# Reordering the opening of a fused attention and feed-forward kernel: two weights loaded and converted ahead of k and v

## The chip, the cores and the metric

The kernel runs on one core of a Trainium2 chip. The metric is the device time of one execution in microseconds. Before the change the median of three runs is 1489.09 us (1489.03 to 1489.66).

## The reference

Three layers follow one another on 4608 tokens (8 batches of 576) of width 512 (8 heads of 64), all in fp32:

```
kv  = einsum('bhsd,bhse->bhde', k, v)            # one 64x64 matrix per batch and head
out = einsum('bhsd,bhde->bhse', q, kv)
x   = out / sqrt(mean(out*out, -1) + 1e-6) * g_norm      # per token and head
h   = maximum(maximum(x @ w1, x @ w2), x @ w3)           # 512 -> 768
x   = h @ w_out                                          # 768 -> 512
xn  = x / sqrt(mean(x*x, -1) + 1e-6) * rms_g
y   = (silu(xn @ w_gate) * (xn @ w_val)) @ w_out2        # 512 -> 1536 -> 512
```

## The kernel before, in words

Tokens are worked in nine tiles of 512, called t, each cut into four token tiles of 128, called i (token tiles 0 to 3 make t = 0, 4 to 7 make t = 1). Every large product is made of three fp32r products (high x high, high x low, low x high), so each weight and each activation is held as a high and a low part. A unit of the second layer, `proj`, is 4 x 3 products of 512 columns into one PSUM bank.

The weights arrive as raw 64-bit words of 512 KB for each 128x512 block, and are converted on the core. One conversion, `convert1`, runs through these steps; a generator's `yield` stands between two of them:

1. `conv_a` (lines 90 to 99): a clip of the high words on VectorE or GpSimd (line 96; which one is chosen by the running number `n` of the conversion), and a copy of the low words on ScalarE (line 97).
2. A scaling on ScalarE (line 116).
3. A shift on VectorE (line 120).
4. Two VectorE passes, the sign and the sum with the low words (lines 122 and 123).
5. A copy on ScalarE, which gives the high part (line 126).
6. A subtraction on VectorE, which gives the low part (line 128).

`convert` has the same work in fewer steps and gives the last subtraction to GpSimd (lines 81 and 82, 101, 107 to 109); `convert2` likewise (lines 239 to 246). The list `todo` holds the weights in the order w1, w2, w3 of block j = 0, the same of j = 1 and then the block 0 of `wo`, and so on. `start` issues the load of the next one on SP's queue and puts it in `flight`; `pump` takes every weight in flight one step further and starts one more. `con(c0, c1, ...)` takes the named ones one step each.

A token tile has five steps (`token_steps`, called by `go((i, step), ...)`):

0. Products of q with the batch's k-v matrix on TensorE (line 367), squares on ScalarE (line 373).
1. Sums of the squares by head on VectorE (line 377), their mean (line 379), and the power -1/2 on GpSimd (line 381).
2. The scaling of the products, `xn`, on VectorE (line 344).
3. Four transposes on TensorE (line 387) and the high part of x on ScalarE (line 388).
4. The low part of x on VectorE (line 393).

`do_kv(b)` makes the k-v matrices of batch b from four chunks of 128 tokens and a tail of 64 (line 332), and copies them out of PSUM on VectorE (lines 336 and 337). Its argument `idle` and the function `busy` put products of the identity on TensorE that nothing reads (line 315).

`do_p(t, j, mid, p, last)` makes one hidden block of 128 rows: three units with the weights w1, w2, w3 of block j; a copy of the first on ScalarE (line 437), a max on VectorE after the second and the third (lines 441 and 445), and the split of the hidden block (ScalarE line 428, GpSimd line 429). `mid` is called after the first and after the second unit, `last` at the end: that is where the token steps and the conversions of other tiles are written in. `do_o` multiplies a hidden block with a block of `wo`.

The order of the instructions on every engine is that of the program text (`manual_schedule`); an engine waits at the head of its list. The opening, from line 992 on, is written out by hand: k and v of batch 0, q, three weights, k and v of batch 1, q, three weights are loaded; then come the k-v products of batch 0, the tokens 0 to 3 with the conversions of c0, c1, c2 (the three weights of j = 0) between them, the first unit of t = 0 in two halves of 256 tokens (`p0`), and then `do_p(0, 0)`, `do_p(0, 1)`, `do_o`, `do_p(1, 0)`, and a loop over j from 2 on.

Of the kernel before, what the change touches and what calls it, by code (L numbers as in the profile page):

```python
# [18 lines left out]
P = 128  # L19
# [12 lines left out]


@with_exitstack
def tile_kernel(ctx: ExitStack, tc, qT, k, v, gcol, w1, w2, w3, wo, wg, wv, wo2, rmsg, out):
    nc = tc.nc
    w1, w2, w3, wo, wg, wv, wo2 = (w.bitcast(I32) for w in (w1, w2, w3, wo, wg, wv, wo2))

# [14 lines left out]
    def unit(shape, dt, name):  # L53
        return up.tile(shape, dt, tag="u", name=name)
# [35 lines left out]
    def conv_a(raw):  # L90
        lo, hi = raw[:, :, 0], raw[:, :, 1]
        tt = unit([P, 2, 512], F32, "wt")
        n_w[0] += 1
        n = n_w[0]
        eng = nc.gpsimd if n > 3 and n % 2 else nc.vector
        eng.tensor_scalar(tt[:, 0], f32(hi), TOP, -TOP, ALU.min, ALU.max)
        nc.scalar.activation(tt[:, 1].bitcast(I32), lo.bitcast(U32), AF.Copy, scale=2.0**-29)
        return tt
# [178 lines left out]
    def cols(w, j):  # L277
        return w[j]

    for j in range(J1 + 1):  # L280
        if j < J1:
            todo += [(convert2 if j >= 3 else convert if j else convert1)((1, i, j), cols(w, j)) for i, w in enumerate((w1, w2, w3))]
        if j:
            todo.append((convert2 if j >= 3 else convert)((1, "o", j - 1), wo[(j - 1) * P:j * P, :]))

    KV = {}
    Q = {}
# [2 lines left out]
    def load_kv_part(b, c):  # L290
        r = b * S
        m, tail = KV.setdefault(b, ([None] * 4, []))
        for i, (src, nm) in enumerate(((k, "k"), (v, "v"))):
            if c == 2:
                tail.append(rp.tile([P, 512], F32, tag="raw", name="kvt"))
                nc.sync.dma_start(tail[i][:64], src[r + 512:r + 576, :])
            else:
                m[2 * i + c] = unit([P, 2, 512], F32, nm)
                rows = src[r + 2 * c * P:r + 2 * (c + 1) * P, :]
                nc.sync.dma_start(m[2 * i + c], rows.rearrange("(p two) f -> p two f", two=2))  # L300

    def load_kv(b):
        for c in range(3):
# [13 lines left out]
    def do_kv(b, kvb, idle={}):  # L317
        m, tail = KV.pop(b)
        pk = psum([P, NP, D], "pk")
        for c in range(5):  # L320
            if c in idle:
                busy(idle[c])
            for hp in range(NP):
                for h in range(2):
                    o = (2 * hp + h) * D
                    if c < 4:
                        kk = m[c // 2][:, c % 2, o:o + D]
                        vv = m[2 + c // 2][:, c % 2, o:o + D]
                    else:
                        kk = tail[0][:64, o:o + D]  # L330
                        vv = tail[1][:64, o:o + D]
                    nc.tensor.matmul(  # L332
                        pk[h * D:(h + 1) * D, hp, :], kk, vv,
                        start=(c == 0 and hp == 0), stop=(c == 4), skip_group_check=True,
                    )
        nc.vector.tensor_copy(kvb[:D, :, 0:D], pk[:D])
        nc.vector.tensor_copy(kvb[D:, :, D:], pk[D:])
        kvbd[b] = kvb

    XN = {}  # L340
# [10 lines left out]

    X = {}

    def token_steps(i, pool=ps):

        st = {}

        def products():
            q = Q[i // 2]
            o = (i % 2) * P  # L360
            po = st["po"] = pool.tile([P, DM], F32, tag="ps" if pool is ps else "acc", name="po")
            t0 = i * P
            b = t0 // S
            n = min(P, (b + 1) * S - t0)
            for hp in range(NP):
                f = slice(hp * P, (hp + 1) * P)
                nc.tensor.matmul(po[:n, f], q[:, hp, o:o + n], kvbd[b][:, hp, :], start=True, stop=True)  # L367
                if n < P:
                    nc.tensor.matmul(po[n:, f], q[:, hp, o + n:o + P], kvbd[b + 1][:, hp, :], start=True, stop=True)
            if i % 2:  # L370
                del Q[i // 2]
            st["sq"] = tmp("sq")
            nc.scalar.activation(st["sq"], po, AF.Square)

        def scales():
            ss = sp.tile([P, H], F32, tag="ss", name="ss")
            nc.vector.tensor_reduce(ss, st["sq"].rearrange("p (h d) -> p h d", h=H), AX.X, ALU.add)
            ms = sp.tile([P, H], F32, tag="ms", name="ms")
            nc.vector.tensor_scalar(ms, ss, 1.0 / D, EPS, ALU.mult, ALU.add)  # L379
            st["rs"] = sp.tile([P, H], F32, tag="rs", name="rs")  # L380
# [609 lines left out]
                pass  # L990

    with tc.manual_schedule():
        load_kv(0)
        load_q(0)
        load_q(1)
        for _ in range(3):
            start(todo[0])
        nc.sync.dma_start(gc, gcol)
        load_kv(1)
        load_q(2)  # L1000
        load_q(3)
        for _ in range(3):
            start(todo[0])
        make_identity(nc, ident)
        nc.gpsimd.memset(mhalf, -0.5)
# [2 lines left out]
        z = unit([P, 2, NP, P], F32, "kvbd")  # L1008
        nc.gpsimd.memset(z, 0.0)
        kvb += [z[:, 0], z[:, 1]]  # L1010
        c0, c1, c2 = flight[:3]
        tok = [token_steps(i) for i in range(NS)] + [token_steps(i, pa) for i in range(NS, 2 * NS)]

        def go(*steps):
            for i, n in steps:
# [3 lines left out]
            for g in gs:  # L1019
                next(g, 0)  # L1020

        do_kv(0, kvb[0], {0: 11, 2: 6})
        busy(4)
        new_x(0)
        go((0, 0), (1, 0), (0, 1), (1, 1), (2, 0))
        con(c0)
        go((3, 0))
        con(c0)
        go((2, 1), (0, 2))
        busy(8)  # L1030
        go((0, 3))
        con(c0, c0)
        go((1, 2), (3, 1))
        busy(5)
        go((1, 3))
        con(c1, c0)
        go((0, 4), (1, 4))
        con(c0, c1)
        p0 = pa.tile([P, TB], F32, tag="acc", name="p0")
        half = TB // 2  # L1040
        busy(4)
        proj(p0, W[1, 0, 0], X[0], 0, half)
        go((2, 2), (3, 2), (2, 3), (3, 3))
        busy(3)
        con(c1, c1)
        go((2, 4), (3, 4))
        con(c1, c2, c1, c2, c2, c2, c2, c2)
        proj(p0, W[1, 0, 0], X[0], half, TB)
        del flight[:3]
        pump(2)  # L1050
        nc.sync.dma_start(gb, rmsg)

        n_mid = [0]

        def mid():
            n_mid[0] += 1
            if n_mid[0] == 1:
                do_kv(1, kvb[1])
                pump()
            elif n_mid[0] == 2:  # L1060
                pump()
                go((4, 0), (5, 0), (4, 1), (5, 1))
            elif n_mid[0] == 3:
                go((6, 0), (7, 0))
            elif n_mid[0] == 4:
                go((4, 2), (6, 1), (5, 2), (7, 1))
                pump()
            elif n_mid[0] == 5:
                go((4, 3), (6, 2))
            else:  # L1070
                go((4, 4), (5, 3), (7, 2), (6, 3))


        do_p(0, 0, mid, p0, mid)
        new_x(1)
        do_p(0, 1, mid, None, mid)
        do_o(1, 0, 0, J1, lambda: go((7, 3), (5, 4), (6, 4), (7, 4)))
        pump()
        do_p(1, 0, pump)

        def pumped():
            tick()
# [123 lines left out]
                down(n, ph, xs)  # L1206


_INS = ["qT", "k", "v", "gcol", "w1", "w2", "w3", "wo", "wg", "wv", "wo2", "rmsg"]


# [34 lines left out]
```

## Time and profile before

| | before |
|---|---|
| median of 3 runs | 1489.09 us |
| profiled execution, its own time | 1492.71 us |
| span of the profiled execution | 1490.7 us |
| TensorE busy | 1472.2 us (99%) |
| VectorE busy | 951.2 us (64%) |
| ScalarE busy | 574.5 us (39%) |
| GpSimd busy | 527.1 us (35%) |
| mean rate of the DMA queues | 211 GB/s |

The busy time of TensorE counts every product, also the ones that nothing reads. The time of an execution is a little longer than its span, and the profiled execution is longer than the median of the runs. In the profile PE is TensorE, DVE is VectorE, ACT is ScalarE, POOL is GpSimd and SP is SyncE, whose queue issues the loads and stores. A clock of 1.00 is 2.4 GHz at TensorE, 0.50 is 1.2 GHz.

### The profile page before, as it was taken

How to read it: one execution, taken by the hardware profiler on the slowest of the kernel's cores; microseconds unless marked ns; L12 is line 12 of the kernel's file. 1: busy time of each engine (PE TensorE's matmuls, PEld its weight loads, DVE VectorE, ACT ScalarE, POOL GpSimd, SP SyncE). 2: the span in 40 equal slices, each digit the busy share in tenths (PEclk: the TensorE clock that was granted, in tenths of full speed). 3: DMA queues.
4: the chain of work that ended last, by engine and by line, in shares of the span. 5: the costliest groups of instructions: out<-in, count | busy, mean ns of one | idle time of the engine just before them, and what ended most of it. 6: DMA issues, size and time to landing. Idle time of an engine off the chain costs nothing.

```text
span 1490.7 us, 20078 instructions
## 1 busy us (share of the span) xinstructions
PE 1472.2 (99%) x7282; PEld 1221.9 (82%) x7282; DVE 951.2 (64%) x1376; ACT 574.5 (39%) x1027; POOL 527.1 (35%) x402
## 2 busy tenths in 40 slices
PE   8899999999999999999999999999999999999998
PEld 7788888888888878888888888888888888888887
DVE  5895476798777966832353655764756656755756
ACT  3553343444343524321232442443333432434432
POOL 2554234334343434311141422532424422443323
PEclk9999999999999999999999999999999999999999
DMA  9323244677547664517695843784657844775442
GB/s 353 104 67 133 65 155 170 219 256 256 201 161 263 245 222 161 192 56 295 240 364 190 329 171 127 303 327 175 242 193 285 304 187 186 282 265 215 179 173 107
DMA packets 104866, 313.80 MB, mean 211 GB/s; under 512 B 11840, under 2 KB 11840, under 8 KB 104768
## 3 DMA queue, kind: packets, MB, share of 16 engines
q1 hardware_dynamic: 104768, 312.52, 57.2%
q8 instruction: 58, 0.95, 0.3%
q14 instruction: 40, 0.33, 0.1%
HBM read 239.08 MB, written 73.40 MB: 210 GB/s over the span
## 4 chain that ended last, share of the span: by engine, by line
PE 92%; DVE 4%; DMA 1%; issue 1%; POOL 1%; ACT 1%; SPq 0%; DVEq 0%; POOLq 0%
PE ua L789 18%; PE da L789 9%; PE ub L789 9%; PE p L410 9%; PE p L412 9%; PE p L411 9%; PE db L789 4%; PE uc L789 4%; PE acc L412 4%; PE acc L410 4%; PE acc L411 4%; PE dc L789 2%; PE po L367 2%; PE pk L332 1%; PE pt L387 1%
## 5 line engine op out<-in xcount | busy, mean ns | idle before, releaser
L410 PE MATMUL p<-x,w 128*128 128x512 f32 (+1 forms) x652 | 257.7, 395 | 1.6 <-ACT w L126 1.0
L411 PE MATMUL p<-x,w 128*128 128x512 f32 (+1 forms) x652 | 253.3, 389 | 1.6 <-DVE x L393 1.6
L412 PE MATMUL p<-x,w 128*128 128x512 f32 (+1 forms) x652 | 253.8, 389 | 0.2 <-DVE w L128 0.2
L789 PE MATMUL ua<-xo,w 128*128 128x512 f32 x864 | 213.4, 389 | 0.0
L429 POOL TENSOR_TENSOR ho<-sl,ho 128x512 fp32r<-128x512 f32 x72 | 98.1, 1369 | 303.3 <-issue 265.0
L789 PEld LDWEIGHTS ua<-xo,w 128*128 128x128 f32 x864 | 162.2, 188 | 33.6
L429 POOL TENSOR_TENSOR hs<-h,hs 128x512 fp32r<-128x512 f32 x54 | 75.8, 1403 | 292.5 <-ACT hs L428 276.5
L429 POOL TENSOR_TENSOR ho<-t,ho 128x512 fp32r<-128x512 f32 x96 | 123.8, 1293 | 133.1 <-ACT ho L428 116.1
L789 PE MATMUL ub<-xo,w 128*128 128x512 f32 x576 | 146.1, 389 | 0.0
L411 PEld LDWEIGHTS p<-x,w 128*128 128x128 f32 x652 | 122.6, 188 | 26.6 <-DVE x L393 2.6
L412 PEld LDWEIGHTS p<-x,w 128*128 128x128 f32 x652 | 122.4, 188 | 26.7 <-POOL w L246 0.4
L410 PEld LDWEIGHTS p<-x,w 128*128 128x128 f32 x652 | 122.5, 188 | 26.4 <-ACT w L126 1.1
L789 PEld LDWEIGHTS ub<-xo,w 128*128 128x128 f32 x576 | 108.1, 188 | 22.4
L871 ACT ACTIVATE s<-ua 128x512 f32<-128x512 f32 x96 | 57.2, 596 | 139.1 <-PE ua L789 139.0
L789 PE MATMUL da<-ho,wd 128*128 128x512 f32 x432 | 105.7, 389 | 0.0
L381 POOL TENSOR_TENSOR rs<-ms,mhalf 128x8 f32<-128x8 f32 x36 | 64.2, 1794 | 105.0 <-DVE ms L379 104.8
L428 ACT ACTIVATE ho<-t 128x512 fp32r<-128x512 f32 x96 | 59.4, 627 | 100.5 <-DVE t L623 100.5
L428 ACT ACTIVATE hs<-h 128x512 fp32r<-128x512 f32 x54 | 34.1, 632 | 163.5 <-DVE h L445 148.7
L789 PEld LDWEIGHTS da<-ho,wd 128*128 128x128 f32 x432 | 81.1, 188 | 16.8
L441 DVE TENSOR_TENSOR s<-p,s 128x512 f32<-128x512 f32 x54 | 37.2, 688 | 83.0 <-PE p L412 83.0
L819 DVE TENSOR_TENSOR c<-uc,s 128x512 f32<-128x512 f32 x48 | 33.1, 690 | 83.8 <-PE uc L789 83.8
L410 PE MATMUL acc<-hs,w 128*128 128x512 f32 x216 | 85.6, 396 | 0.0
(147 smaller groups left out, 2828.2 us busy)
## 6 DMA issues: line engine op xcount, KB each, us to landing
w<-wd SPq DMA_DIRECT2D x180, 512.0 KB, 8.0
wd<-ws SPq DMA_DIRECT2D x72, 512.0 KB, 3.0
wd<-wd SPq DMA_DIRECT2D x72, 512.0 KB, 7.4
wq<-wd SPq DMA_DIRECT2D x72, 256.0 KB, 8.3
xo<-td SPq DMA_DIRECT2D x32, 512.0 KB, 9.6
q<-in_qT SPq DMA_DIRECT2D x18, 512.0 KB, 5.5
raw<-in_w SPq DMA_DIRECT2D x18, 512.0 KB, 9.0
raw<-in_wo SPq DMA_DIRECT2D x18, 512.0 KB, 5.1
```

The lines of the kernel that those rows point to most:

```text
L332: nc.tensor.matmul(pk[h * D:(h + 1) * D, hp, :], kk, vv, start=(c == 0 and hp == 0), stop=(c == 4), skip_group_check=True,)
L367: nc.tensor.matmul(po[:n, f], q[:, hp, o:o + n], kvbd[b][:, hp, :], start=True, stop=True)
L381: nc.gpsimd.tensor_tensor(st["rs"], ms, mhalf.to_broadcast([P, H]), ALU.pow)
L410: nc.tensor.matmul(o, ah, bh, start=first, stop=False)
L411: nc.tensor.matmul(o, ah, bl, start=False, stop=False)
L412: nc.tensor.matmul(o, al, bh, start=False, stop=last)
L428: nc.scalar.activation(hs[:, 0], h, AF.Copy)
L429: nc.gpsimd.tensor_tensor(hs[:, 1], h, f32(hs[:, 0]), ALU.subtract)
L441: nc.vector.tensor_tensor(s2, p, s1, ALU.max)
L789: nc.tensor.matmul(o, aa, bb, start=first and q == 0, stop=last and q == 2, skip_group_check=True)
L819: nc.vector.tensor_tensor(t, p, s, ALU.add)
L871: nc.scalar.activation(t, p, AF.Copy)
```

## The change

- The first two weights (c0 and c1) are loaded ahead of k and v of batch 0, and converted ahead of the k-v products. The third follows behind q; four more are loaded behind batch 1 (before: three).
- The 64-token tails of k and v of batches 0 and 1 come in one transfer, `kvt`, a new input of 128 rows of 1024 values that the host lays out; batch 0 uses its partitions 0 to 63, batch 1 the others.
- The k-v matrices are copied out of PSUM by ScalarE, for all batches.
- Token tiles 4 to 7 take their squares head by head, eight ScalarE instructions of 64 columns that also give the sum (`accum_out`), and VectorE's sums are left out for them.
- The weights d0, d1, d2 (j = 1), o0 and p1[0] to p1[2] (j = 2) are `convert1`, and their steps are written out in `mid`, as are those of the token tiles 4 to 7. The first ten conversions clip on VectorE (before: the first three, and every second one after them).
- The k-v products of batch 1 stand ahead of the second half of p0 (before: after it). The first unit of t = 1 is made in two halves, and `do_p(1, 0)` stands ahead of the first `do_o`.
- More products that nothing reads stand ahead of and between the first k-v products.

The diff, without the lines of the host and of the arguments:

```diff
-        eng = nc.gpsimd if n > 3 and n % 2 else nc.vector
+        eng = nc.gpsimd if n > 10 and n % 2 else nc.vector
...
-            todo += [(convert2 if j >= 3 else convert if j else convert1)((1, i, j), cols(w, j)) for i, w in enumerate((w1, w2, w3))]
+            todo += [(convert2 if j >= 3 else convert1)((1, i, j), cols(w, j)) for i, w in enumerate((w1, w2, w3))]
         if j:
-            todo.append((convert2 if j >= 3 else convert)((1, "o", j - 1), wo[(j - 1) * P:j * P, :]))
+            todo.append((convert2 if j >= 3 else convert if j > 1 else convert1)((1, "o", j - 1), wo[(j - 1) * P:j * P, :]))
...
+        if c == 2:
+            if b == 0:
+                t = unit([P, 2, DM], F32, "kvt")
+                nc.sync.dma_start(t, kvt.rearrange("p (two f) -> p two f", two=2))
+                tail += [t[:64, 0], t[:64, 1]]
+                KV[1] = ([None] * 4, [t[64:, 0], t[64:, 1]])
+            elif b > 1:
+                for i, src in enumerate((k, v)):
+                    tail.append(rp.tile([P, 512], F32, tag="raw", name="kvt")[:64])
+                    nc.sync.dma_start(tail[i], src[r + 512:r + 576, :])
+            return
         for i, (src, nm) in enumerate(((k, "k"), (v, "v"))):
-            if c == 2:
-                tail.append(rp.tile([P, 512], F32, tag="raw", name="kvt"))
-                nc.sync.dma_start(tail[i][:64], src[r + 512:r + 576, :])
-            else:
-                m[2 * i + c] = unit([P, 2, 512], F32, nm)
-                rows = src[r + 2 * c * P:r + 2 * (c + 1) * P, :]
-                nc.sync.dma_start(m[2 * i + c], rows.rearrange("(p two) f -> p two f", two=2))
+            m[2 * i + c] = unit([P, 2, 512], F32, nm)
+            rows = src[r + 2 * c * P:r + 2 * (c + 1) * P, :]
+            nc.sync.dma_start(m[2 * i + c], rows.rearrange("(p two) f -> p two f", two=2))
...
-        nc.vector.tensor_copy(kvb[:D, :, 0:D], pk[:D])
-        nc.vector.tensor_copy(kvb[D:, :, D:], pk[D:])
+        nc.scalar.activation(kvb[:D, :, 0:D], pk[:D], AF.Copy)
+        nc.scalar.activation(kvb[D:, :, D:], pk[D:], AF.Copy)
         kvbd[b] = kvb
...
-            st["sq"] = tmp("sq")
-            nc.scalar.activation(st["sq"], po, AF.Square)
+            st["sq"] = sq = tmp("sq")
+            if not sums:
+                nc.scalar.activation(sq, po, AF.Square)
+                return
+            st["ss"] = sp.tile([P, H], F32, tag="ss", name="ss")
+            for h in range(H):
+                f = slice(h * D, (h + 1) * D)
+                nc.scalar.activation(sq[:, f], po[:, f], AF.Square, accum_out=st["ss"][:, h:h + 1])
 
         def scales():
-            ss = sp.tile([P, H], F32, tag="ss", name="ss")
-            nc.vector.tensor_reduce(ss, st["sq"].rearrange("p (h d) -> p h d", h=H), AX.X, ALU.add)
+            if not sums:
+                st["ss"] = sp.tile([P, H], F32, tag="ss", name="ss")
+                nc.vector.tensor_reduce(st["ss"], st["sq"].rearrange("p (h d) -> p h d", h=H), AX.X, ALU.add)
+            ss = st["ss"]
...
     with tc.manual_schedule():
+        for _ in range(2):
+            start(todo[0])
         load_kv(0)
         load_q(0)
         load_q(1)
-        for _ in range(3):
-            start(todo[0])
+        start(todo[0])
         nc.sync.dma_start(gc, gcol)
         load_kv(1)
         load_q(2)
         load_q(3)
-        for _ in range(3):
+        for _ in range(4):
             start(todo[0])
         make_identity(nc, ident)
...
-        c0, c1, c2 = flight[:3]
-        tok = [token_steps(i) for i in range(NS)] + [token_steps(i, pa) for i in range(NS, 2 * NS)]
+        c0, c1, c2, d0, d1, d2, o0 = flight
+        tok = [token_steps(i) for i in range(NS)] + [token_steps(i, pa, True) for i in range(NS, 2 * NS)]
...
-        do_kv(0, kvb[0], {0: 11, 2: 6})
+        con(c0, c0, c1, c0, c1, c0, c0, c1, c1, c0, c1, c1)
+        do_kv(0, kvb[0], {0: 26, 2: 7})
         busy(4)
         new_x(0)
-        go((0, 0), (1, 0), (0, 1), (1, 1), (2, 0))
-        con(c0)
-        go((3, 0))
-        con(c0)
-        go((2, 1), (0, 2))
-        busy(8)
+        go((0, 0), (1, 0), (0, 1), (1, 1), (2, 0), (3, 0), (2, 1), (0, 2))
+        con(c2)
+        go((3, 1))
+        busy(6)
         go((0, 3))
-        con(c0, c0)
-        go((1, 2), (3, 1))
+        con(c2)
+        go((1, 2), (0, 4))
         busy(5)
-        go((1, 3))
-        con(c1, c0)
-        go((0, 4), (1, 4))
-        con(c0, c1)
+        go((1, 3), (2, 2), (1, 4))
+        busy(3)
+        go((2, 3))
         p0 = pa.tile([P, TB], F32, tag="acc", name="p0")
         half = TB // 2
-        busy(4)
         proj(p0, W[1, 0, 0], X[0], 0, half)
-        go((2, 2), (3, 2), (2, 3), (3, 3))
-        busy(3)
-        con(c1, c1)
-        go((2, 4), (3, 4))
-        con(c1, c2, c1, c2, c2, c2, c2, c2)
+        go((3, 2), (2, 4))
+        con(c2)
+        go((3, 3))
+        do_kv(1, kvb[1])
+        go((3, 4))
+        con(c2, c2)
         proj(p0, W[1, 0, 0], X[0], half, TB)
-        del flight[:3]
-        pump(2)
-        nc.sync.dma_start(gb, rmsg)
-
+        con(c2, d0)
+        go((4, 0), (5, 0))
+        del flight[:]
         n_mid = [0]
+        p1 = []
 
         def mid():
             n_mid[0] += 1
-            if n_mid[0] == 1:
-                do_kv(1, kvb[1])
+            n = n_mid[0]
+            if n == 1:
+                con(d0, d0)
+                go((4, 1), (5, 1))
+                con(d0, d0)
+            elif n == 2:
+                con(d0, d1, d1)
+                go((6, 0), (7, 0))
+                con(d1, d1, d1)
+                for _ in range(3):
+                    start(todo[0])
+                p1.extend(flight)
+                del flight[:]
+            elif n == 3:
+                con(d1, d2, d2)
+                go((6, 1), (7, 1))
+                con(d2, d2, d2)
+                nc.sync.dma_start(gb, rmsg)
+            elif n == 4:
+                con(d2)
+                new_x(1)
+                go((4, 2), (5, 2))
+                start(todo[0])
+            elif n == 5:
+                go((4, 3), (5, 3), (6, 2), (7, 2), (4, 4), (5, 4))
+                con(o0, o0)
+                start(todo[0])
+            elif n == 6:
+                go((6, 3), (7, 3), (6, 4), (7, 4))
+                con(o0, o0, o0)
+                start(todo[0])
+            elif n == 7:
+                con(o0, p1[0], p1[0], p1[0], p1[0], p1[0])
                 pump()
-            elif n_mid[0] == 2:
+            elif n == 8:
+                con(p1[0], p1[1], p1[1], p1[1], p1[1], p1[1])
                 pump()
-                go((4, 0), (5, 0), (4, 1), (5, 1))
-            elif n_mid[0] == 3:
-                go((6, 0), (7, 0))
-            elif n_mid[0] == 4:
-                go((4, 2), (6, 1), (5, 2), (7, 1))
+            else:
+                con(p1[1], p1[2], p1[2], p1[2], p1[2], p1[2])
                 pump()
-            elif n_mid[0] == 5:
-                go((4, 3), (6, 2))
-            else:
-                go((4, 4), (5, 3), (7, 2), (6, 3))
-
 
         do_p(0, 0, mid, p0, mid)
-        new_x(1)
         do_p(0, 1, mid, None, mid)
-        do_o(1, 0, 0, J1, lambda: go((7, 3), (5, 4), (6, 4), (7, 4)))
+        p0 = pa.tile([P, TB], F32, tag="acc", name="p0")
+        proj(p0, W[1, 0, 0], X[1], 0, half)
+        proj(p0, W[1, 0, 0], X[1], half, TB)
+        do_p(1, 0, mid, p0, mid)
+        do_o(1, 0, 0, J1, lambda: con(p1[2]))
         pump()
-        do_p(1, 0, pump)
```

## Rows read from the trace of the kernel before

**Rows 1.** Windows: start:end, length, busy (x instructions) by engine, PEclk, DMA share, GB/s.
```profile
0.00:35.77 35.77, 29.50 (x315) 27.63 (x315) 17.34 (x33) 11.80 (x20) 10.19 (x14) 0.90 0.98 351
35.77:60.00 24.23, 20.13 (x118) 16.14 (x114) 22.14 (x38) 13.18 (x25) 13.52 (x10) 1.00 0.38 133
60.00:80.00 20.00, 19.95 (x89) 16.24 (x90) 15.05 (x20) 10.22 (x19) 9.88 (x9) 1.00 0.25 80
```
**Rows 2.** Chain of waits in order of time: start, duration, what.
```profile
3.17 8.33 DMA kvt<-in_v
11.64 1.12 PE pk L332 x16
```
**Rows 3.** Timeline of TensorE: start, duration, line, operation, [idle before, releaser].
```profile
5.72 1.15 PE L332 MATMUL pk<-v,k 128*64 128x64 f32 x32
...
10.28 1.15 PE L332 MATMUL pk<-v,k 128*64 128x64 f32 x32 [1.87 <-DMA v<-in_v]
...
14.56 5.52 PE L367 MATMUL po<-kvbd,q 128*128 128x128 f32 x32
...
33.14 2.08 PE L332 MATMUL pk<-v,k 128*64 128x64 f32 x64
...
35.77 0.50 PE L410 MATMUL p<-x,w 128*128 128x512 f32 x1
...
43.49 1.95 PE L367 MATMUL po<-kvbd,q 128*128 128x128 f32 x16
...
53.11 0.66 PE L387 MATMUL pt<-ident,xn 128*128 128x128 f32 x4 [2.23 <-DVE xn L344]
```
**Rows 4.** Windows within the first 19 us.
```profile
8.00:9.00 1.00, 0.41 (x4) 0.22 (x2) 0.00 (x0) 0.00 (x0) 0.00 (x0) 1.00 1.13 209
9.00:10.00 1.00, 0.00 (x0) 0.00 (x0) 0.00 (x0) 0.00 (x0) 0.00 (x0) 1.00 0.97 295
12.00:13.00 1.00, 1.00 (x16) 0.88 (x14) 0.12 (x1) 0.00 (x0) 0.00 (x0) 0.50 1.03 414
18.50:19.00 0.50, 0.50 (x7) 0.50 (x6) 0.15 (x1) 0.31 (x1) 0.50 (x1) 1.00 1.00 401
```
**Rows 5.** Windows, the stage of tokens 0 to 3.
```profile
22.00:24.00 2.00, 1.48 (x14) 1.29 (x12) 1.97 (x4) 0.69 (x1) 1.42 (x1) 1.00 1.02 291
```
**Rows 6.** Groups by line of VectorE, 0 to 80 us: count, busy us, mean ns.
```profile
L393 DVE SCALAR_TENSOR_TENSOR x<-pt,gc,x 128x512 fp32r<-128x512 f32 x8 | 5.7, 746 | 0.8 <-ACT x L388 0.7
...
L96 DVE TENSOR_SCALAR wt<-raw 128x512 f32<-128x512 f32 x8 | 3.3, 420 | 0.0
...
L128 DVE TENSOR_TENSOR w<-wt,w 128x512 fp32r<-128x512 f32 x3 | 2.1, 690 | 0.8 <-ACT w L126 0.8
```
**Rows 7.** Groups by line of ScalarE, whole span.
```profile
L97 ACT ACTIVATE wt<-raw 128x512 int32<-128x512 uint32 x60 | 39.4, 660 | 1.3 <-PE acc L412 1.3
...
L210 ACT ACTIVATE ws<-wt 128x512 fp32r<-128x512 f32 x60 | 36.6, 624 | 0.0
...
L373 ACT ACTIVATE sq<-po 128x512 f32<-128x512 f32 x36 | 21.2, 593 | 45.5 <-PE po L367 43.0 <-PE po L369 2.5
...
L210 ACT ACTIVATE ws<-wt 128x256 fp32r<-128x256 f32 x24 | 8.5, 405 | 0.0
...
L1006 ACT ACTIVATE ones<-ident 128x128 fp32r<-128x128 f32 x1 | 0.3, 311 | 0.0
```
**Rows 8.** Timelines of GpSimd, VectorE and ScalarE.
```profile
18.19 5.23 POOL L381 TENSOR_TENSOR rs<-ms,mhalf 128x8 f32<-128x8 f32 x3 [15.97 <-DVE ms L379]
...
27.19 1.28 DVE L344 TENSOR_TENSOR xn<-po,rs 128x512 f32<-128x512 f32 x2
...
30.09 0.69 POOL L96 TENSOR_SCALAR wt<-raw 128x512 f32<-128x512 f32 x1 [3.48 <-DMA raw<-in_w]
...
35.41 1.80 ACT L97 ACTIVATE wt<-raw 128x512 int32<-128x512 uint32 x3
...
60.58 1.29 POOL L429 TENSOR_TENSOR hs<-h,hs 128x512 fp32r<-128x512 f32 x1
```
**Rows 9.** Timeline of TensorE near 90 us.
```profile
90.38 0.39 PE L410 MATMUL p<-x,w 128*128 128x512 f32 x1
```

More of the change, by code (lines that the diff above doesn't have):

```diff
@@ L34, in tile_kernel @@
 @with_exitstack
-def tile_kernel(ctx: ExitStack, tc, qT, k, v, gcol, w1, w2, w3, wo, wg, wv, wo2, rmsg, out):
+def tile_kernel(ctx: ExitStack, tc, qT, k, v, kvt, gcol, w1, w2, w3, wo, wg, wv, wo2, rmsg, out):
     nc = tc.nc
@@ L329, in do_kv @@
                     else:
-                        kk = tail[0][:64, o:o + D]
-                        vv = tail[1][:64, o:o + D]
+                        kk = tail[0][:, o:o + D]
+                        vv = tail[1][:, o:o + D]
                     nc.tensor.matmul(
@@ L352, in tile_kernel, with token_steps @@
     X = {}
-    def token_steps(i, pool=ps):
+    def token_steps(i, pool=ps, sums=False):
         st = {}
@@ L1206, in tile_kernel @@
                 down(n, ph, xs)
-_INS = ["qT", "k", "v", "gcol", "w1", "w2", "w3", "wo", "wg", "wv", "wo2", "rmsg"]
+_INS = ["qT", "k", "v", "kvt", "gcol", "w1", "w2", "w3", "wo", "wg", "wv", "wo2", "rmsg"]
 def kernel(q, k, v, g_norm, moe_w1, moe_w2, moe_w3, moe_w_out, moe2_w_gate, moe2_w_val, moe2_w_out, moe2_rms_g):
@@ L1220, in by_column, with tails @@
         return lay(w.reshape(KC, P, -1, P).transpose(2, 1, 0, 3).reshape(-1, P, DM))
+    def tails(a):
+        rows = np.transpose(a[:2], (0, 2, 1, 3)).reshape(2, S, DM)[:, S // P * P:]
+        return rows.reshape(P, DM)
     arrays = {
@@ L1225 @@
         "v": lay(np.transpose(v, (0, 2, 1, 3)).reshape(NT, DM)),
+        "kvt": lay(np.concatenate([tails(k), tails(v)], axis=1)),
         "gcol": lay(np.concatenate([g_norm, g_norm]).reshape(P, 1)),
```

## The prediction, made before the changed kernel was run

> **What bounds the kernel now.** I read the windows of busy time first. Past 60 us TensorE is busy for 19.95 of 20 us and little but matmul work decides; before that it is busy for 29.50 of 35.77 us and then 20.13 of 24.23 [rows 1]. All that the change moves lies in the first 90 us, so only this opening can win or lose, and what it loses is not made up, because TensorE has no slack behind it.
>
> The chain of waits then says what holds the opening up. The tail of v lands at 11.50 us, and the k-v products end 1.1 us later [rows 2]. The token products start at 14.56 and four of them take 5.52 us, where two later ones take 1.95 [rows 3]: the granted clock stood at 0.50 (1.2 GHz) at 12 us, after 1.87 us in which TensorE waited for v, and was back at 1.00 by 18.5 [rows 3, 4]. From 22 us on VectorE is the limit: 1.97 us busy of 2.00 while TensorE has 1.48 [rows 5]. It does the first weights' conversions in between the tokens' own work. The second weight's projection begins at 35.77 us [rows 3]. In 35.77 to 60 TensorE loses another 4.1 us [rows 1], half of it in one wait of 2.23 us of a transpose for VectorE [rows 3].
>
> **The change part by part.** Durations are those of the profiled execution (span 1490.7, its own time 1492.7; the median of the runs is 1489.1, 3.6 lower, so the difference found here is added to either). I walk the new order down each engine: an instruction starts when its engine is free and its operands are there. A VectorE pass of 512 columns takes 0.69 to 0.75 us, the clip or shift 0.42 [rows 6], a ScalarE pass 0.59 to 0.66 [rows 7] and 0.60 apart (three in 1.80) [rows 8]. The same walk down the old order ends tile 1's second unit at 89.8 us; in the trace the next product starts at 90.38 [rows 9].
>
> *Loads.* Two raw weights (1.05 MB) go ahead of k and v on SP's queue. At the 0.41 MB/us of a full microsecond [rows 4] that is 2.6 us. One tail transfer of 0.52 MB replaces two of 0.13 MB now and two later: 0.65 us more ahead of the products. Around the old tails the queue moved only 209 and 295 GB/s [rows 4], some 0.3 MB less than full rate; full-width rows should give 0.8 us back. The tail lands at 11.5+2.6+0.65-0.8 = 14.0 us. Everything behind it on SP (q, the third weight, batch 1, the next four) has the same bytes ahead of it, or fewer. Without the 0.8, or with all four tails' loss returned, it is 14.8 or 13.2.
>
> *First conversions.* c0 and c1 take k's and v's place at the head of the queue, whose first products start at 5.72 us [rows 3]; so they have landed by then, and each needs some 4.2 us of VectorE and ScalarE in turn. They are done by about 11 us. What hides them is the loading of k and v until 14.0; were it gone, up to 5 us would come onto the path. Gone from the path are 2 x (0.42+0.42+0.69+0.69+0.69) = 5.8 us of VectorE in the stage that it limits.
>
> *Clock.* The filling products (26 more, and 7 between the halves) keep TensorE at work up to each landing, so I expect full clock: four token products in 3.5 us instead of 5.5.
>
> *k-v copies on ScalarE.* About 0.4 us each against VectorE's 0.42 and 0.43; ScalarE idles there, so nothing either way. For batch 1 they stand ahead of c2's copy, inside the half-projection's 1.4 us; the six later batches' copies lie beside dense products.
>
> Together: token products from 15.9 to 19.4, four pow steps on GpSimd at 1.74 each (three in 5.23 [rows 8]) until 25.3, the fourth tile's x ready at 28.5, batch 1's k-v products (2.6 us, from 33.14 to the projection at 35.77 [rows 3]) inside that wait, the second half-projection done at 30.9. The old order has the same work behind it at 35.8 (36.3 by the walk): a lead of 5.4.
>
> *The eight tiles and seven weights from there.* Each conversion is now run as one block: clip, ScalarE's scale, shift, two VectorE passes, ScalarE's copy, and the last subtraction on VectorE in the next block. VectorE stands still for the scale (0.7), so a block with its max costs it 0.42+0.7+0.42+0.7+0.7+0.7+0.7 = 4.4 us, while TensorE's unit of twelve products takes 2.7. VectorE has no lead at 30.9. The old weights ended on GpSimd and ran several abreast. Loads are no term here: the next three weights are issued in the second step, some 25 us before use. The waits this makes, in order:
>
> - Tokens 4 to 7 take 8 squares of 64 columns with a sum each. No such instruction is in the trace. ScalarE's 512, 256 and 128 columns take 0.62, 0.405 and 0.311 [rows 7], so 64 take about 0.264 by the last step's slope. Below, they overlap as the long ones do (0.17 apart); above, the sum is a second instruction of the same length (0.53). I take 0.264, the nearest row's duration without overlap: 2.1 us a token instead of 0.59, for 0.69 of VectorE saved.
> - d0's scale stands behind sixteen of them and a copy on ScalarE, so VectorE idles 5 us before d0's shift; d0 is ready at 41.1, wanted at 39.8: 1.3.
> - d1's copy stands behind the squares of tokens 6 and 7: ready at 48.0, wanted at 43.9: 4.1.
> - The transposes of token 4 wait for its scaling, which is behind d2 on VectorE: 3.3 with token 5's.
> - The last tokens' low parts: 2.0.
> - p1 (the third unit's second weight): 0.8.
> - p2: its clip is the thirteenth and goes to GpSimd, behind the last max's subtraction there (1.29, then 0.69 [rows 8]). Its last subtraction on VectorE is written behind another weight's three passes. Wanted at 77.6, ready at 84.7: 7.1.
>
> Sum 18.6, where the old order waits 4.6 by the walk (4.1 in the trace). So -5.4 + 18.6 - 4.6 = +8.6. With VectorE's independent passes 0.60 apart, as two in 1.28 have it [rows 8], the walk gives +7.7. I take +8: 1497, or 1500.7 in an execution under the profile. At 0.17 a square it is +5, at 0.53 +17; a landing 0.8 earlier or later moves each by as much.
>
> The Trainium skill (ScalarE: Activation LUTs, What ACT_TABLE_LOAD costs) states 186 ns plus 0.833 ns a column for an ACTIVATE, overlapping by 93 when back to back. By that, squares would be 0.146 apart and the sum of the walk about +4.4, or 1493.5; it states no price for the sum, and no row here shows one.
>
> **The rivals.**
> *The lead is kept (faster).* VectorE's plain work from 30.9 to p2 is seven conversions of 2.9 (20.6 with c2's end, less p2's clip), six maxes (4.1), eight scalings and low parts (5.7), tokens' means (0.7) and the next weights' first passes (3.1): 34 us. TensorE's is nine units (24.5), tokens (5.2), one half-and-half projection (2.8) and an output block (2.7): 35. If the two pass work to and fro with less standing than I count (squares near 0.17, blocks overlapping), the waits stay at the old 4.6 and only the lead counts: 1489.1 - 5.4 = 1483.7. For it: the two sums are even, and the saved 5.8 us lie where VectorE is full [rows 5]. Against it: every wait above follows from the written order. It decides if p2 is ready within 2 us of being wanted.
> *Lead and waits cancel (no change).* Squares at 0.17 take 3.1 off the waits, and blocks that overlap half of those for p2 and token 4 (5.2): -5.4 + 10.3 - 4.6 = 0.3, so 1489. For and against it stands what was said of the rival before; it holds if p2 is some 3 us late.
> *Worse.* The sum is a second instruction, +17, or a 7 us stand for p2 lets the granted clock fall. In the old opening it was at half for some 6.5 us after 1.87 us of waiting [rows 3, 4], which costs half of that, 3.3; the 2.23 us near 51 did not lower it. With the forecast's waits that is 1500, with the second instruction 1506.
>
> **How the numbers follow.** Forecast 0.56 (own range 1492.5 to 1500), worse 0.10, lead kept 0.19, cancelled 0.15. A measurement of this kernel tells about 0.2% (3 us) from no change. Faster 0.19, same 0.15, slower 0.66. The range 1483.5 to 1503.5 takes in the faster rival's value and the lower part of the worse one.
>
> **What would show it.** Right: the second half-projection ends near 31 us; clock 1.00 throughout 10 to 30; 32 small squares of tokens 4 to 7, about 0.26 each, with VectorE idle for some 5 us around 33 to 37; TensorE waits for d1 near 44 to 48 and for p2 near 78 to 85. Wrong: the opening no shorter (k, v too late, or a cold clock); squares of 0.17 apart or less; TensorE dense from 45 us on; or p2's clip not behind the max on GpSimd.

## The result and the profile after

The changed kernel takes 1499.45 us, the median of 6 runs (1498.58 to 1500.5), against 1489.41 for the kernel before (6 runs, 1489.03 to 1489.78): a ratio of 1.0068, 95% interval 1.0055 to 1.0081. It is slower by some 10 us. Its profiled execution took 1499.37 us, with a span of 1497.6, where the one of before had 1490.7.

The windows of busy time of the changed kernel (columns as in [rows 1]):

```profile
0.00:31.20 31.20, 29.46 (x334) 27.88 (x334) 16.43 (x31) 13.68 (x24) 8.08 (x12) 1.00 0.97 378
31.20:60.00 28.80, 23.48 (x130) 19.27 (x129) 17.93 (x33) 17.67 (x83) 10.10 (x7) 0.94 0.44 157
52.00:55.00 3.00, 3.00 (x12) 2.71 (x11) 3.00 (x6) 1.93 (x3) 0.00 (x0) 0.50 0.53 175
60.00:80.00 20.00, 16.24 (x74) 13.01 (x73) 12.62 (x23) 9.79 (x18) 2.35 (x3) 0.97 0.17 53
79.00:85.00 6.00, 3.81 (x8) 2.60 (x9) 5.32 (x8) 4.31 (x8) 2.12 (x2) 0.50 0.24 77
100.00:150.00 50.00, 50.00 (x294) 41.58 (x293) 33.28 (x42) 19.18 (x34) 23.44 (x17) 1.00 0.31 100
```

The opening to 31.2 us does what the old one did to 35.77. Then TensorE loses 5.3 us of 28.8 and 3.8 of the next 20, where it lost 4.1 and nothing [rows 1]. VectorE has 17.9 of 28.8 and 12.6 of 20: it isn't full, it stands as well. Twice the granted clock is at 0.50 (1.2 GHz). From 100 us on TensorE is dense again.

TensorE's timeline says where (start, duration, line, operation, idle before and its releaser):

```profile
14.04 0.68 PE L339 MATMUL pk<-kvt 64*64 64x64 f32 x16
...
15.70 3.81 PE L374 MATMUL po<-kvbd,q 128*128 128x128 f32 x32
...
33.15 0.47 PE L425 MATMUL p<-x,w 128*128 128x512 f32 x1
...
51.70 1.97 PE L402 MATMUL pt<-ident,xn 128*128 128x128 f32 x8 [3.46 <-DVE xn L351]
...
59.70 0.39 PE L425 MATMUL p<-x,w 128*128 128x256 f32 x1 [0.30 <-ACT x L403]
60.57 0.39 PE L426 MATMUL p<-x,w 128*128 128x256 f32 x1 [0.48 <-DVE x L408]
...
79.05 0.80 PE L425 MATMUL p<-x,w 128*128 128x512 f32 x1 [3.27 <-ACT w L126]
...
82.42 0.79 PE L427 MATMUL p<-x,w 128*128 128x512 f32 x1 [2.15 <-DVE w L128]
...
86.33 0.40 PE L425 MATMUL acc<-hs,w 128*128 128x512 f32 x1
```

The tail's products run at 14.04, four token products take 3.81 us instead of 5.52 [rows 3], the second weight's projection starts at 33.15 (35.77 before). One wait more, 1.57 us at 44.96 for ScalarE's copy of d1, isn't shown. The last row is the second output block; by then both kernels have done the same work. It starts at 79.50 in the shown execution of before, so 6.8 us are lost there, and the spans differ by 6.9.

How the wait for p2 (`p1[2]` of the diff, the third weight of j = 2) comes about, on GpSimd and on VectorE:

```profile
73.86 1.29 POOL L444 TENSOR_TENSOR hs<-h,hs 128x512 fp32r<-128x512 f32 x1 [13.40 <-ACT hs L443]
75.12 0.64 POOL L96 TENSOR_SCALAR wt<-raw 128x512 f32<-128x512 f32 x1
```
```profile
76.45 0.43 DVE L120 TENSOR_SCALAR wt<-wt 128x512 int32<-128x512 int32 x1 [3.67 <-ACT wt L116]
76.91 0.69 DVE L122 SCALAR_TENSOR_TENSOR wt<-raw,wt 128x512 int32<-128x512 int32 x1
77.64 0.69 DVE L123 CUSTOM_DVE_ANT_0 wt<-wt 128x1024 uint16<-128x1024 uint16 x1
79.54 0.43 DVE L107 TENSOR_SCALAR wt<-wt 128x512 int32<-128x512 int32 x1 [1.21 <-ACT wt L101]
80.01 0.69 DVE L108 SCALAR_TENSOR_TENSOR wt<-raw,wt 128x512 int32<-128x512 int32 x1
80.73 0.69 DVE L109 CUSTOM_DVE_ANT_0 wt<-wt 128x1024 uint16<-128x1024 uint16 x1
81.34 0.42 DVE L96 TENSOR_SCALAR wt<-raw 128x512 f32<-128x512 f32 x1
81.68 0.68 DVE L128 TENSOR_TENSOR w<-wt,w 128x512 fp32r<-128x512 f32 x1
```

On GpSimd the clip (L96) stands behind the last max's subtraction, which comes late: the engine had been idle for 13.40 us before it. VectorE then stands 3.67 us, runs p2's passes (L120 to L123), then three passes and a clip of other weights (L107 to L109, L96), and only then p2's low part (L128).

### The profile page after: what moved, and what is told of

Its sections match the earlier page's. It is cut to its first block, busy times and chain, and to the rows that moved or that the text cites. A ratio compares the mean times of both kernels' runs of the same rounds, so it can differ in the third digit from the quotient of the medians.

```text
span 1497.6 us, 20176 instructions
## 1 busy us (share of the span) xinstructions
PE 1476.3 (99%) x7314; PEld 1225.3 (82%) x7314; DVE 942.3 (63%) x1366; ACT 586.3 (39%) x1103; POOL 514.9 (34%) x392
## 4 chain that ended last, share of the span: by engine, by line
PE 92%; DVE 3%; issue 2%; POOL 1%; ACT 1%; DMA 1%; SPq 0%; POOLq 0%; DVEq 0%; ACTq 0%
PE ua L804 17%; PE da L804 9%; PE ub L804 9%; PE p L425 8%; PE p L427 8%; PE p L426 8%; PE db L804 4%; PE uc L804 4%; PE acc L425 4%; PE acc L426 4%; PE acc L427 4%; PE dc L804 2%; PE po L374 2%; PE pk L339 1%; PE pt L402 1%
## 5 line engine op out<-in xcount | busy, mean ns | idle before, releaser
L425 PEld LDWEIGHTS p<-x,w 128*128 128x128 f32 x656 | 124.1, 189 | 30.9 <-ACT w L126 5.7
L427 PEld LDWEIGHTS p<-x,w 128*128 128x128 f32 x656 | 123.7, 189 | 29.3 <-DVE w L128 3.3
L426 PEld LDWEIGHTS p<-x,w 128*128 128x128 f32 x656 | 124.1, 189 | 26.5 <-DVE x L408 2.5
```

Source lines behind the costliest of these rows:

```text
L425: nc.tensor.matmul(o, ah, bh, start=first, stop=False)
L426: nc.tensor.matmul(o, ah, bl, start=False, stop=False)
L427: nc.tensor.matmul(o, al, bh, start=False, stop=last)
```

## The experiments

Each is compared with the kernel before on the same chip. "Block" is the start of the second output block in its profile, "waits" are TensorE's of 0.2 us and more from 31 to 90 us. In the filled kernel the filling products count as work, so its 3.2 is not what it loses.

| kernel | median us | ratio to before (95%) | block | waits |
|---|---|---|---|---|
| before, shown / looked at again | 1489.41 / 1490.45 (one run) | | 79.50 / 76.88 | 4.8 / 2.3 |
| changed | 1499.45 | 1.0068 (1.0055 to 1.0081) | 86.33 | 11.2 |
| p2 early | 1496.87 | 1.0045 (1.003 to 1.006) | 81.72 | 7.6 |
| one square a token | 1498.42 | 1.0057 (1.004 to 1.0074) | 84.72 | 9.9 |
| front only | 1491.02 | 1.0006 (0.9996 to 1.0015) | 78.17 | 6.0 |
| old, kept warm | 1490.24 | 1.0003 (0.9994 to 1.0013) | 76.69 | 2.6 |
| changed, filled | 1497.25 | 1.0052 (1.004 to 1.0065) | 83.16 | 3.2 |
| interleaved | 1491.51 | 1.0011 (1.0002 to 1.002) | 78.41 | 5.6 |
| interleaved, sums | 1491.79 | 1.0012 (1.0003 to 1.0021) | 78.65 | 5.7 |
| reordered | 1483.82 | 0.9961 (0.9948 to 0.9973) | 70.92 | 0.6 |
| reordered, second | 1483.56 | 0.9954 (0.994 to 0.9968) | 70.24 | 0.3 |

But for p2 early, blocks and medians tell the same: each median is within 1 us of 1490.0 (before, beside the experiments, had 1489.9 to 1490.1) plus its block less 76.88.

**p2 early**: p2's low part is taken in the ninth call of `mid`, ahead of the other weights' steps, and its clip on VectorE (with that of the eleventh conversion).

```diff
-        eng = nc.gpsimd if n > 10 and n % 2 else nc.vector
+        eng = nc.gpsimd if n > 13 and n % 2 else nc.vector
...
-                con(p1[1], p1[2], p1[2], p1[2], p1[2], p1[2])
+                con(p1[1], p1[2], p1[2], p1[2], p1[2], p1[2], p1[2])
...
-        do_o(1, 0, 0, J1, lambda: con(p1[2]))
+        do_o(1, 0, 0, J1)
```

> From the changed kernel: p2's last subtraction stands directly behind its copy, ahead of the other weights' steps, and the first thirteen clips are on VectorE, so p2's clip no longer stands behind the max's subtraction on GpSimd. Theory (p2 is late by written order): TensorE waits for it until about 78.1 us instead of 82.4, the clock does not fall to half at 79 to 85, and the kernel takes 1499.4 - 5.5 = 1494. Rival (VectorE's whole load sets the pace, the order does not matter): the weights behind it come late instead, and it takes 1498 to 1500.

Measured 1496.87, 2.6 less than the changed kernel and between the theory's 1494 and the rival's 1498. The wait for p2 is 1.84 instead of 5.42 us, but the clock fell even so:

```profile
77.01 0.50 PE L425 MATMUL p<-x,w 128*128 128x512 f32 x1 [1.84 <-ACT w L126]
```
```profile
78.00:80.00 2.00, 2.00 (x6) 1.53 (x6) 1.93 (x5) 1.58 (x4) 0.00 (x0) 0.50 0.10 12
```

The block is 4.6 us earlier, of which 2.6 are left in the time. At the fourth output block 3.3 are left (121.12 us against 124.45): two waits for VectorE, 0.7 in all, have come up where the changed kernel has none, and VectorE is nearly full there in both (14.69 and 14.73 of the 15 us from 85 on). Where the rest goes is not shown.

**One square a token**: tokens 4 to 7 with one square and VectorE's sum, as before the change.

```diff
-        tok = [token_steps(i) for i in range(NS)] + [token_steps(i, pa, True) for i in range(NS, 2 * NS)]
+        tok = [token_steps(i) for i in range(NS)] + [token_steps(i, pa) for i in range(NS, 2 * NS)]
```

> From the changed kernel: tokens 4 to 7 take one square of 512 columns on ScalarE and the sums on VectorE again. Theory: ScalarE is free 1.0 us earlier per token, which d0 and d1 gain (TensorE's 1.6 us wait for d1 falls to about 0.4), and VectorE's four sums of 0.69 take it back at token 4's scaling: 1499 to 1500, no change. Rival (the squares on ScalarE are what makes the weights late): 3 us or more faster, 1496 or less.

Measured 1498.42, 1.0 less than the changed kernel. The wait for d1 is gone, so the squares were its cause; those for token 4 (3.51) and p2 (3.28 and 2.34) stay. The squares carry about a tenth of the loss.

**Front only**: the new opening up to the second half-projection, then the old order, with the old clips, conversions and squares (those lines left out).

```diff
-        con(c2, d0)
-        go((4, 0), (5, 0))
-        del flight[:]
+        con(c2)
+        del flight[:3]
+        pump(2)
...
+            elif n_mid[0] == 2:
...
+                go((4, 0), (5, 0), (4, 1), (5, 1))
+            elif n_mid[0] == 3:
+                go((6, 0), (7, 0))
+            elif n_mid[0] == 4:
+                go((4, 2), (6, 1), (5, 2), (7, 1))
...
+        do_o(1, 0, 0, J1, lambda: go((7, 3), (5, 4), (6, 4), (7, 4)))
```

> The changed kernel up to the second half-projection, and from there the old order (conversions of j = 1 and 2 by pump with the last subtraction on GpSimd, one square and VectorE's sums, first output block ahead of the second tile). Theory (the opening gives a lead of 4.5 us, the rest loses it): the lead is kept, 1489.4 - 4.5 = 1485. Rival (VectorE's conversions set the pace from 31 us on, so a lead of TensorE is only waited away): 1488 to 1490.

Measured 1491.02: the rival was right. The second weight's projection starts at 30.59, and 21 us later the whole lead is gone, in one wait:

```profile
51.64 1.11 PE L402 MATMUL pt<-ident,xn 128*128 128x128 f32 x4 [6.04 <-DVE xn L351]
```

VectorE was nearly full for 15 us before it (13.93 us busy from 36 to 51), and one of its passes over two operands takes longer while GpSimd subtracts:

```profile
37.00 1.66 DVE L109 CUSTOM_DVE_ANT_0 wt<-wt 128x1024 uint16<-128x1024 uint16 x1
...
39.75 1.66 DVE L109 CUSTOM_DVE_ANT_0 wt<-wt 128x1024 uint16<-128x1024 uint16 x1
...
47.57 0.69 DVE L109 CUSTOM_DVE_ANT_0 wt<-wt 128x1024 uint16<-128x1024 uint16 x1
```
```profile
36.70 1.40 POOL L82 TENSOR_TENSOR w<-wt,w 128x512 fp32r<-128x512 f32 x1 [4.85 <-ACT w L81]
39.40 1.46 POOL L82 TENSOR_TENSOR w<-wt,w 128x512 fp32r<-128x512 f32 x1 [1.29 <-ACT w L81]
```

Begun under a subtraction of 1.40 to 1.47 us the pass takes 1.66, three times in a row, else 0.69. A pass of two operands that had begun before the subtraction (L108 at 36.27) kept its 0.69. The Trainium skill (GPSIMD Engine Reference, Specifications) says that GpSimd's SBUF interfaces are shared with VectorE and contend with its instructions that have two SBUF inputs; this trace agrees for L109. A shift of one operand (L107 at 45.39) took 1.09 instead of 0.42 under the fourth subtraction as well.

**Old, kept warm**: the kernel before with 14 filling products for 6 between the first two and the last two of the four 128-token chunks.

```diff
-        do_kv(0, kvb[0], {0: 11, 2: 6})
+        do_kv(0, kvb[0], {0: 11, 2: 14})
```

> The old kernel with 14 filling products instead of 6 between the first two pairs of k-v chunks, so TensorE does not wait 1.9 us near 9. Theory (the half clock costs part of the old opening): the granted clock stays at 1.00, four token products take 3.6 us instead of 5.5, and about 1.2 us of it come through, 1488.2. Rival (VectorE sets that stage, so the clock is hidden): 1489.4 with the clock at 1.00.

Measured 1490.24, no change. Its span is 1488.4 and its clock does not fall in the opening, but its median is that of the kernel before. Hence the next.

**Before, looked at again**, unchanged:

> The kernel before, unchanged, for a second look at its opening. Theory: the half clock at 12 to 18 us in the shown profile, and so 2.8 us of the lead that the prediction counted, belong to that one execution and not to most (a version with more filling products, which kept the clock up, had a span of 1488.4 us and the same median). Then the granted clock in 13 to 18 us is 1.00 here, the second weight's projection starts at about 33 us and not at 35.8, and the span is near 1488. Rival: every execution opens as the shown one did: clock 0.50 in 13 to 18, the projection at 35.8, span 1490.7.

The span is 1488.5, and the opening is not the one of [rows 3, 4]:

```profile
10.61 1.15 PE L332 MATMUL pk<-v,k 128*64 128x64 f32 x32 [1.45 <-DMA v<-in_v]
...
13.88 3.81 PE L367 MATMUL po<-kvbd,q 128*128 128x128 f32 x32
...
33.49 0.50 PE L410 MATMUL p<-x,w 128*128 128x512 f32 x1
...
50.51 0.66 PE L387 MATMUL pt<-ident,xn 128*128 128x128 f32 x4 [1.90 <-DVE xn L344]
```
```profile
13.00:18.00 5.00, 5.00 (x45) 4.86 (x45) 3.02 (x8) 2.36 (x5) 1.27 (x1) 1.00 1.04 406
50.00:55.00 5.00, 4.49 (x15) 3.64 (x16) 4.81 (x10) 3.63 (x7) 5.00 (x4) 0.66 0.00 0
```

After 1.45 us of waiting for v, not 1.87, the clock held, and the second weight's projection started 2.3 us earlier. The profile that the prediction worked from showed an execution with a slow opening. That is not the usual one: the 49 executions of the kernel before that ran beside the experiments have spans of 1486.5 to 1489.6 us, and none reaches the 1490.7 of the shown one. Their openings were not looked at one by one. As the usual opening keeps its clock anyway, the kernel kept warm could show no gain, whichever of its two theories holds. Here the clock fell later, after the wait of 1.90 us at 50.51.

**Changed, filled**: 15 filling products ahead of token 4's transpose, 24 ahead of the unit that waits for p2, in a tile of their own.

```diff
+    def fill(n):
+        o = psum([P, P], "fill")
+        for _ in range(n):
+            nc.tensor.matmul(o, ident, ident, start=True, stop=True)
...
             elif n == 5:
+                fill(15)
...
-            do_p(0, j, pumped)
+            do_p(0, j, (lambda: (pumped(), HT.get("f") and fill(24), HT.update(f=True))) if j == 2 else pumped)
```

> The changed kernel with filling products (128 columns, their result unused) where TensorE waits: 15 ahead of token 4's transpose near 48 us, 24 ahead of the unit that waits for its weight at 75.6 us. The waits stay, the clock does not fall. Theory (each fall of the clock costs TensorE time of its own, 1.2 us near 52 and 2.2 us near 80): the clock stays at 1.00, 3 us less than the changed kernel, 1496 to 1497. Rival (the half clock costs nothing because the work behind it waits anyway): the changed kernel's 1499.4 or, where the fillers end late, up to 1501.

Measured 1497.25, 2.2 less than the changed kernel, 0.8 short of the expected 3. The clock is at 1.00 in the stretches where it had been at half:

```profile
48.00:53.00 5.00, 4.88 (x40) 4.42 (x39) 4.27 (x7) 2.03 (x4) 2.23 (x2) 1.00 0.23 61
74.00:80.00 6.00, 5.95 (x51) 5.51 (x49) 3.84 (x7) 3.58 (x7) 0.11 (x1) 1.00 0.02 6
80.00:85.00 5.00, 4.23 (x19) 3.51 (x20) 4.88 (x7) 3.06 (x6) 2.44 (x3) 1.00 0.31 105
```

So of the 10 us lost, some 2 by the median and 3 at the second output block come from the clock that falls after the waits, not from the waits themselves.

**Interleaved**: the changed front, tokens and weights, with several conversions abreast, three clips more and two last subtractions on GpSimd, one square a token. Its core:

```diff
+    CLIP = [(1, 2, 1), (1, 0, 2), (1, 1, 2), (1, 2, 2)]
+    LOW = [(1, 2, 1), (1, 'o', 0)]
...
-                con(d1, d2, d2)
-                go((6, 1), (7, 1))
-                con(d2, d2, d2)
+                con(o0, d2)
+                go((5, 2))
+                con(p1[0], d0)
+                go((7, 0), (7, 1), (6, 3))
+                con(p1[0])
+                go((5, 3))
+                con(d2, p1[1], d2)
+                go((7, 2))
+                con(o0)
+                go((4, 3), (4, 4))
+                con(p1[2], p1[2])
+                go((5, 4))
+                con(o0)
+                go((6, 4))
+                con(d2, p1[1], o0, p1[0])
```

> The changed kernel with the same weights and tokens, in another written order from 25 us on: several conversions abreast, the products, means, scalings and conversions of tokens 4 to 7 drawn forward, the clips of four weights and the last subtraction of two on GpSimd, one square per token. Theory (the waits follow from the order of whole conversions one after another, not from VectorE's work): no wait of TensorE over 1.3 us between 31 and 90 us and the clock never at half there; the third weight column's last unit ends about 14 us earlier than in the changed kernel, so about 1485 us (1483.5 to 1487), 4 to 5 below the kernel before. Rival (VectorE's work sets the pace whatever the order, as it looked where only the front was changed): waits of 3 to 6 us in all turn up elsewhere, 1489 to 1491.

Measured 1491.51: 8 us less than the changed kernel, but not below the one before. On balance nothing was moved off VectorE: clips of 0.42 and subtractions of 0.69 saved it 2.6 us, four sums of 0.68 came back. So these 8 us come from the order. Besides a wait of 1.35 us for a scaling at 42.60, one long wait is left, of a kind that the walk hadn't counted:

```profile
50.66 0.79 PE L428 MATMUL p<-x,w 128*128 128x512 f32 x1 [4.20 <-DVE x L411]
```
```profile
49.86 2.06 DVE L411 SCALAR_TENSOR_TENSOR x<-pt,gc,x 128x512 fp32r<-128x512 f32 x3
```

A projection of tile 0 needs no low part (L411) of tile 1's tokens. What it needs is a PSUM tile: projections and transposes share four that go round, and the next was held by a transpose until its low part had been read out, behind conversions on VectorE. ScalarE has a copy that ends at the same time (50.61), but it is that of o0, which this unit does not read. The rival's number came close to true; the last two experiments say whether its reason did.

**Interleaved, sums**: the same with the sums on ScalarE for tokens 4 to 7.

```diff
-        tok = [token_steps(i) for i in range(NS)] + [token_steps(i, pa, i in []) for i in range(NS, 2 * NS)]
+        tok = [token_steps(i) for i in range(NS)] + [token_steps(i, pa, i in [4, 5, 6, 7]) for i in range(NS, 2 * NS)]
```

> The interleaved order with the eight squares and sums of each of tokens 4 to 7 on ScalarE, as the changed kernel has them. Theory: 16 us of ScalarE's time less 2.1 saved on VectorE is no gain in an order without slack on ScalarE near 35 us: some 1.5 us more than the interleaved order with one square, of it a longer wait for the first column's third weight near 38 us, and up to 1.2 more if that wait lets the clock fall: 1486 to 1488. Rival (VectorE is the engine that counts, so its 0.69 us a token come back): 1.5 to 2.7 us less than the interleaved order.

Measured 1491.79, the same within the intervals. Neither the loss of 1.5 nor the gain of 1.5 came; the wait for the round of PSUM tiles is there in both (3.85 here, 4.20 before). The 16 us of ScalarE's time in the expectation are too many: 32 squares at the changed kernel's 0.197 are 6.3.

**Reordered**, and **reordered, second**: the walk now counts the PSUM round; the last low parts come ahead of the third column's conversions. The core of the first:

```diff
+                go((4, 2), (6, 3))
+                con(d1)
+                go((5, 2))
+                con(o0)
+                go((7, 3))
+                con(p1[2], p1[2])
+                go((6, 4))
+                con(d2)
+                go((4, 3))
+                con(p1[0])
+                go((7, 4))
             elif n == 5:
-                go((4, 3), (5, 3), (6, 2), (7, 2), (4, 4), (5, 4))
-                con(o0, o0)
-                start(todo[0])
+                pump()
+                con(p1[2])
+                go((4, 4), (5, 3), (5, 4))
+                con(p1[1], p1[1], p1[0], o0, p1[2])
```

> The changed kernel's weights and tokens in a third written order from 25 us on. The order before it left one wait of 4.20 us, of a unit of the second column for a low part of tokens 4 to 7: the four PSUM tiles that projections and transposes share go round, and a projection got the tile that a transpose still held until its low part was done. Here the low parts of the last tokens come ahead of the conversions of the third column's weights and of the next projection in that round; clips of five weights and the last subtraction of four are on GpSimd; tokens 4 and 5 have the sums on ScalarE. Theory (the front's lead of about 2 us is real and every wait behind it follows from the written order): by the walk with the PSUM tiles counted no wait over 0.6 us from 31 to 90 us, tile 1's second unit done at 79.7 where the kernel before has 87.6 in its usual opening: 1481 to 1485 us, below the kernel before by 5 to 8. Rival (VectorE's work is the pace; each order moves its waits to another place): again a wait of 3 to 5 us and 1489 to 1491.

> A fourth order, found from another start, with the same rule for the low parts: clips of four weights and the last subtraction of six on GpSimd. Theory: as the third order, within 1 us of it (tile 1's second unit done at 80.2 by the walk), with one wait of some 0.5 us of the second column's last unit for a low part: 1481.5 to 1486. Rival: six subtractions on GpSimd slow VectorE's two-operand passes more than the walk has it, and the waits come back: 1487 to 1491.

Measured 1483.82 and 1483.56: 6 us below the kernel before and 16 below the changed one, with the same front, weights and tokens. Windows of the second:

```profile
35.00:60.00 25.00, 24.74 (x133) 21.12 (x132) 23.21 (x38) 17.04 (x58) 16.97 (x13) 1.00 0.42 157
60.00:80.00 20.00, 20.00 (x89) 16.32 (x89) 18.40 (x23) 12.20 (x22) 11.36 (x9) 1.00 0.26 79
```

TensorE is dense with the clock at 1.00; VectorE has 23.2 of 25 us where the changed kernel had 16.9 of the same 25. Six subtractions on GpSimd made single passes of VectorE longer (1.78 instead of 0.69 at 57.82) but brought no wait back. The theory, that the order makes the waits, holds, with one reserve: more clips and subtractions went to GpSimd here and two tokens' sums came back, which takes some 3 and 4 us net off VectorE by the lengths of its passes. That is an estimate, and far from the 16.

## Why the prediction was right, and where it was not

The forecast was 1497 and slower; it came out 1499.45, inside its own range and nearer to the worse rival's 1500. The mechanism is the one predicted: the written order makes waits that cost more than the opening gains. That the sum came so near is in part luck. The lead, the waits of both orders and the squares were mis-sized, the clock's fall was left out, and the errors nearly cancelled.

- *Loads, clock and copies*: right. The tail was to land at 14.0; its products ran at 14.04. The clock held, 3.81 us for four token products against 3.5 forecast. The second half-projection was to end at 30.9 and ended at 31.2.
- *The lead of 5.4*: mis-sized. It was taken from the walk's 36.3; in the shown executions it is 35.77 - 31.21 = 4.6, and against the usual opening 33.49 - 31.21 = 2.3. The step that failed is the one that said the 3.6 us between the shown execution and the median could be "added to either": 2.2 of them lay in the very stage that was being improved. The forecast took credit for mending a slow opening that the usual execution does not have.
- *The waits, 18.6*: too many. They are 11.2. d1 took 1.57 instead of 4.1, d0 and p1 had none, the last tokens' high and low parts 0.8 instead of 2.0, p2 5.4 instead of 7.1; token 4 was right (3.46 for 3.3). The old order's 4.6 are 2.3 in the execution looked at again.
- *The squares*: 0.264 forecast, and 16 take 32.41 to 35.56, 0.197 each, nearer the lower bound of 0.17. By the prediction's own steps (+8 at 0.264, +5 at 0.17) that is about +6, so the wrong size brought the forecast nearer to the result:

```profile
32.41 0.22 ACT L386 ACTIVATE sq<-po 128x64 f32<-128x64 f32 x1 [0.70 <-PE po L376]
32.53 0.19 ACT L386 ACTIVATION_READ_ACCUMULATOR sq<-po 128x1 f32 x1
32.62 0.21 ACT L386 ACTIVATE sq<-po 128x64 f32<-128x64 f32 x1
```

  The sum is a second instruction, as the upper bound had it, but the two overlap: one starts every 0.098 us. By the Trainium skill (ScalarE: Activation LUTs, What ACT_TABLE_LOAD costs) 64 columns take an estimated 0.239 us; 0.21 to 0.22 at the start of the row of squares is close (the last ones of the row are 0.33 long). VectorE's stand behind them was right, 4.63 us for 5:

```profile
36.83 0.43 DVE L120 TENSOR_SCALAR wt<-wt 128x512 int32<-128x512 int32 x1 [4.63 <-ACT wt L116]
```

- *The clock in the waits*: left out of the sum, kept for the worse rival. It fell twice. Near 52 us eight transposes and a unit took 1.62 and 3.62 us where later ones take 0.79 and 2.72, so 1.7 more. After p2's wait products stood 0.43 apart instead of 0.23, which cost some 2.4: 79.05 to 86.33 is 7.28, less the wait of 2.15 and the 2.72 of a unit. That is 4.1; the filled kernel gets 3.2 of it back at the second block and 2.2 in time. The old order's clock falls once: from its transpose to the second block it takes 25.96 us without the waits in the execution looked at again, and 24.47 in the shown one, where the clock held: 1.5.
- Put together, for the usual opening: -2.3 of lead, +11.2 of waits and +4.1 of clock, less the 2.3 that the order before waits and the 1.5 of its clock: +9.2. The second output blocks lie 9.45 apart (86.33 and 76.88), the fourth 9.2 (124.45 and 115.25); the medians lie 10.0 apart.
- *Two readings*: the edit has 26 filling products for 11, not "26 more", and three ScalarE passes in 1.80 us, the last of 0.66, are 0.57 apart, not 0.60. Both are small.
- *The rival "lead kept"* failed for this order. Its price of 1483.7 is what the reordered kernels take (1483.6 and 1483.8), but by other terms: it had a lead of 5.4 and the old waits kept, where the second reordered kernel has a lead of 2.3 against the usual opening, waits 2.0 us shorter in all and no fall of the clock (1.5): 5.8 of the 6.6 us between the blocks (76.88 and 70.24). Its reason stood: VectorE's and TensorE's work are about even (23.2 and 24.7 of 25 us), if VectorE need not stand.
- *"Lead and waits cancel"* is what the front alone did, for another reason: there VectorE was nearly full.

## What to carry to other kernels

Where two engines have about the same work in a stage, the written order decides: run several conversions abreast, so that one's step on ScalarE lies under another's on VectorE, and put first what frees a shared buffer. Before an opening is improved, profile it twice and compare the spans with those of the other runs: time that is lost in the one profiled execution and not in the usual one is no gain to be had. Count a wait of TensorE with the half clock that may follow it, and count the tiles that go round among its operands.

## What was not expected of the hardware

A fall of the granted clock followed TensorE's waits of 1.84 us (p2 early), 1.90 and 2.21 (the old order near 50 us, looked at again and kept warm), 3.46, 4.20 and 6.04; none followed 1.45 and 1.57. Near 2 us it goes either way: 1.87 at 10 us in the shown execution had one, 2.23 at 53 us in the same one had none. A square of 64 columns with its sum is two records, 0.098 us apart.
